# A packed attention followed by a gated feed-forward on one core: the first batch's steps in another order, 99 copies and splits on other engines, and the first softmax's sums in two-column operations

## The chip, the cores and the metric

The kernel runs as one launch on one core of a Trainium2 chip. The core has five engines that matter here: TensorE (PE in the rows, with its weight loads as PEld), VectorE (DVE), ScalarE (ACT), GpSimd (POOL), and SyncE (SP), which issues the DMAs. Each engine works through its own list of instructions in order and waits for the others by semaphores. The metric is the device time of an execution in microseconds; lower is better. The kernel before takes 666.89 us, the median of three runs (666.89 to 667.42).

## The reference

All arrays are float32: 8 batches, 8 heads, 576 positions, 64 channels per head, 32 packed positions, 2048 hidden features.

```python
scale = 1.0 / np.sqrt(q.shape[-1])
def sm_attn(qq, kk, vv):
    s = scale * np.matmul(qq, kk.transpose(0, 1, 3, 2))
    s = s - np.max(s, axis=-1, keepdims=True)
    a = np.exp(s)
    a = a / (np.sum(a, axis=-1, keepdims=True) + 1e-09)
    return np.matmul(a, vv)
p_packed = sm_attn(p, k, v)
out = sm_attn(q, p_packed, p_packed)          # 8 x 8 x 576 x 64
x = out.transpose(0, 2, 1, 3).reshape(8 * 576, 512)
h = x @ w_in                                  # 512 -> 2048
g = h * (1.0 / (1.0 + np.exp(-1.702 * h)))
return g @ w_out                              # 2048 -> 512
```

## The kernel before, in words

**Precision.** The large products need more than one pass of the fast format. An operand is split into an upper half (a copy rounded to fp32r) and a lower half (the difference), and each product is made of three matmuls: upper by upper, upper by lower, lower by upper. The steps whose names end in `_upper` and `_lower` make these halves: an upper half is a copy by `move` (L178 on ScalarE, L180 on the other engines), a lower half is a subtraction (L300 for w_out, L612 for M, L699 for A, L763 and L869 for the hidden features).

**The work of one batch.** `scores1` multiplies p by k (L376), a softmax over the keys follows, its result is turned (for batch 0 by TensorE, L472 and L484, for later batches by VectorE and through a scratch array `aside` in DRAM, `turn1_out` L501 and `turn1_in` L512), and `pack` multiplies it by v (L525; for batch 0 `pack_first`, L545). `scores2_mm` multiplies q by the packed result (L631); its softmax over the 32 packed positions is done on turned blocks (`scores2_turn` L639, `max2` L656, `sub2` L662, `exp2` L666, `sum2` L670 to L672, `norm2` L676, `turn2` L679) and its weights, split, are A (`a_upper`, `a_lower`; for the first part of batch 0 by TensorE and the copies `a_lower_mm`, L692 and L693). `m_chunk` (L597) multiplies the packed result by a chunk of w_in and gives M; `h_mm` (batch 0) and `hp_mm` (later) multiply M by A (L713) and give the hidden features. The gate is `h_tanh` and `h_gate` (L729, L706) for the first four feature blocks and `h_gelu` (L736) or `hp_gelu` (L829) from then on; `out_mm` (L768, batch 0) and `plain` and `product` (L895, later) multiply by w_out into the four accumulators acc.

**The first batch also decodes the weights.** They arrive as 64-bit integers of which the kernel loads the upper words (`load_w`, L266, on SP's queue); `begin_w` (ScalarE, L274) and `join_w` (VectorE, L287) put a float32 together. w_in takes 16 such blocks (numbers 0 to 3, 8 to 11, 16 to 19, 24 to 27), w_out 16 (the others); the first four blocks are loaded in halves. A block's place is loaded again with a later block once it is joined, so `load_w` waits for `join_w`.

**Banks.** PSUM has eight banks: four accumulators acc0 to acc3, h4 and h5 for `h_mm` in turn, and b6 and b7 for the rest. An `h_mm` into a bank waits until the gate of the `h_mm` before it has read that bank.

**What sets the order.** Nothing is scheduled: one tuple named `order` lists 3649 steps in program order, and each step emits its instructions on the engine that it names, or on its default. An engine's list is this tuple restricted to it. Every engine runs ahead of the others as far as its waits allow. The steps `warm` are matmuls of the identity into an unused bank; they keep TensorE at work while nothing else is ready.

**The first softmax.** It takes its maximum over the first 256 keys first, exponentiates these with that maximum (`exp1_first`), corrects by a factor exp(first maximum minus final maximum) (`factor_first`, L431), and `sum1` joins the two partial sums for each of the two head sets eo = 0 and 1:

```python
sm, rs = sm1(eo), rs1(eo)
if b == 0:
    nc.vector.scalar_tensor_tensor(
        sm[:, 0:1], sm[:, 0:1], ff(eo)[:, 0:1], sm[:, 1:2], op0=ALU.mult, op1=ALU.add
    )
nc.vector.tensor_scalar(rs, sm[:, 0:1], 1e-9, 2.0, op0=ALU.add, op1=ALU.mult)
nc.vector.reciprocal(rs, rs)
if b == 0:
    nc.vector.tensor_scalar(ff(eo)[:, 1:2], ff(eo)[:, 0:1], rs, None, op0=ALU.mult)
```

Of the kernel before, what the change touches and what calls it, by code (L numbers as in the profile page):

```python
# [24 lines left out]
def kernel(  # L25
# [527 lines left out]
    def pack_first_half(eo):  # L553
        t = st["bank", "Pf", 0]
        nc.scalar.activation(
            pf[:, eo, :], t[:, eo * D : (eo + 1) * D], AF.Copy, scale=ff(eo)[:, 1:2]
        )
# [393 lines left out]
    def keep_over(n, i, k, engine=nc.sync):  # L951
# [13 lines left out]
        (factor_first, 0), (turn1_first_copy, 0, dve), (factor_first, 1), (exp1_first, 1, 1),  # L965
        (load_w, 2, 1), (sum1, 0, 1), (turn1_first, 1, 7), (load_w, 3, 1), (sum1, 0, 0),
        (turn1_last_mm, 0, 6), (load_w, 4), (turn1_first_copy, 1), (pack_first, 0),
        (turn1_last_copy, 0), (pack_first, 1), (pack_first_half, 0), (pack_first_half, 1),
        (pack_first, 2), (load, 'k', 1, 0), (pack_first_end, 0), (pack_turn_mm, 0, 7),
        (warm, 6, 2, 5), (pack_turn_copy, 0, act), (begin_w, 0, 0), (load_w, 1, 1),  # L970
        (scores2_mm, 0, 0, (6, 7)), (join_w, 0, 0), (warm, 4, 2, 4), (begin_w, 2, 0),
        (load_w, 0, 1), (scores2_turn, 0, 0, 0), (scores2_mm, 0, 1, (2, 3)),
        (scores2_turn, 0, 0, 1), (begin_w, 1, 0), (load, 'k', 1, 1), (max2, 0, 0, 0),
        (warm, 5, 2, 5), (max2, 0, 0, 1), (warm, 8, 3, 4), (load_w, 7), (scores2_turn, 0, 1, 0),
        (sub2, 0, 0, 1, pool), (scores2_turn, 0, 1, 1), (warm, 0, 3, 5), (load_w, 5),
        (sub2, 0, 0, 0, pool), (max2, 0, 1), (load_w, 9), (warm, 2, 3, 4), (exp2, 0, 0, 0),
        (begin_w, 3, 0), (join_w, 2, 0), (exp2, 0, 0, 1), (join_w, 1, 0), (begin_w, 3, 1),
        (sum2, 0, 0, 0), (load_w, 6), (join_w, 3, 0), (norm2, 0, 0, 0, pool),
        (m_chunk, 0, 0, (0, 1), 0), (sum2, 0, 0, 1), (load_w, 8), (m_upper, 0, 0, 1, 0, act),
        (m_upper, 0, 0, 0, 0, act), (sub2, 0, 1, None, pool), (turn2, 0, 0, 0), (load_w, 11),  # L980
        (m_lower, 0, 0, 1, 0), (a_upper, 0, 0, 0, act), (load_w, 10), (a_lower_mm, 0, 0, 0, 6),
        (norm2, 0, 0, 1, dve), (exp2, 0, 1), (join_w, 3, 1), (scores1, 1, 0, (5, 4)),
        (turn2, 0, 0, 1), (begin_w, 4), (sum2, 0, 1), (load_w, 16), (a_upper, 0, 0, 1, act),
        (a_lower_copy, 0, 0, 0), (a_lower_mm, 0, 0, 1, 7), (scores1_copy, 1, 0, 1, act),
        (join_w, 4), (norm2, 0, 1, None, pool), (m_lower, 0, 0, 0, 0), (upper_w, 4, act),
# [1019 lines left out]
```

## Time and profile before

| what | value |
|---|---|
| median of the three runs | 666.89 us |
| the profiled execution's own time | 665.34 us |
| its span (first to last instruction) | 663.6 us |
| TensorE busy, matmul | 653.4 us (98%) |
| VectorE busy | 497.0 us (75%) |
| ScalarE busy | 375.9 us (57%) |
| GpSimd busy | 240.3 us (36%) |
| granted TensorE clock | 1.0 of full speed in every slice |

A busy share on TensorE includes matmuls whose ends are modelled, so a row that is busy throughout may still hold short waits; a wait of a few tenths of a microsecond shows as a note in brackets behind a row, or as a group of matmuls that takes longer than another group of the same count. The first 25 us hold the loads, the first softmax and the first decoding of weights; from then on the rows of TensorE follow each other.

### The profile page before, as it was taken

How to read it: one execution, taken by the hardware profiler on the slowest of the kernel's cores; microseconds unless marked ns; L12 is line 12 of the kernel's file. 1: busy time of each engine (PE TensorE's matmuls, PEld its weight loads, DVE VectorE, ACT ScalarE, POOL GpSimd, SP SyncE). 2: the span in 40 equal slices, each digit the busy share in tenths (PEclk: the TensorE clock that was granted, in tenths of full speed). 3: DMA queues.
4: the chain of work that ended last, by engine and by line, in shares of the span. 5: the costliest groups of instructions: out<-in, count | busy, mean ns of one | idle time of the engine just before them, and what ended most of it. 6: DMA issues, size and time to landing. Idle time of an engine off the chain costs nothing.

```text
span 663.6 us, 15877 instructions
## 1 busy us (share of the span) xinstructions
PE 653.4 (98%) x6136; PEld 594.1 (90%) x6136; DVE 497.0 (75%) x1078; ACT 375.9 (57%) x735; POOL 240.3 (36%) x319
## 2 busy tenths in 40 slices
PE   8999999999999999999999999999999999999997
PEld 6578777899899988999899998899989998899997
DVE  4988786999996577657887658785788558964685
ACT  4886786557884357725646535663657536523430
POOL 2540441154253335342413143462244434444431
PEclk9999999999999999999999999999999999999999
DMA  8998654625553354625632536363545454210231
GB/s 335 417 385 265 220 195 130 177 76 195 174 154 90 112 198 178 156 48 174 245 122 83 141 112 207 112 186 77 177 143 159 100 164 146 79 39 13 82 117 34
DMA packets 94252, 103.14 MB, mean 155 GB/s; under 512 B 69152, under 2 KB 74208, under 8 KB 89568
## 3 DMA queue, kind: packets, MB, share of 16 engines
q1 hardware_dynamic: 94016, 101.86, 49.0%
q8 instruction: 48, 0.79, 0.5%
q14 instruction: 28, 0.23, 0.1%
q10 hardware_dynamic: 160, 0.26, 0.1%
HBM read 80.14 MB, written 21.95 MB: 154 GB/s over the span
## 4 chain that ended last, share of the span: by engine, by line
PE 89%; DVE 1%; ACT 1%; issue 1%; DVEq 0%; ACTq 0%
PE acc L895 47%; PE hh L713 27%; PE acc L768 5%; PE b L597 4%; PE h L713 2%; PE b L525 1%; PE hh L631 1%; PE hh L376 1%; ACT L187 0%; ACT at_float L829 0%; DVE at_float L925 0%; DVE at_float L938 0%; PE b L376 0%; ACT L666 0%; PE h L631 0%
## 5 line engine op out<-in xcount | busy, mean ns | idle before, releaser
L895 PE MATMUL acc<-at_float32r 128*128 128x256 f32 (+1 forms) x2652 | 353.8, 284 | 0.1
L895 PEld LDWEIGHTS acc<-at_float32r 128*128 128x128 f32 x2652 | 331.9, 189 | 22.1 <-issue 14.2
L713 PE MATMUL hh<-at_float32r 128*128 128x288 f32 x1344 | 206.8, 296 | 0.2
L713 PEld LDWEIGHTS hh<-at_float32r 128*128 128x128 f32 x1344 | 185.5, 188 | 3.8 <-issue 0.9
L178 ACT CAST at_float32r<-at_float 128x512 fp32r<-128x512 f32 (+5 forms) x211 | 117.3, 572 | 75.4 <-PE acc L895 48.6
L869 DVE TENSOR_TENSOR at_float32r<-at_float,at_float32r 128x512 fp32r<-128x512 f32 (+3 forms) x186 | 121.4, 663 | 35.5 <-ACT at_float32r L178 31.4
L829 ACT ACTIVATE at_float<-hh 128x576 f32<-128x576 f32 x112 | 73.0, 651 | 131.8 <-PE hh L713 83.7
L869 POOL TENSOR_TENSOR at_float32r<-at_float,at_float32r 128x416 fp32r<-128x416 f32 (+1 forms) x66 | 80.3, 1219 | 103.9 <-ACT at_float32r L178 58.5
L180 DVE CAST at_float32r<-at_float 128x416 fp32r<-128x416 f32 (+5 forms) x125 | 53.1, 430 | 36.8 <-PE acc L895 28.9
L854 POOL TENSOR_TENSOR at_float<-at_float 128x256 f32<-128x256 f32 x49 | 38.0, 778 | 61.5 <-ACT at_float L829 29.6
L854 DVE TENSOR_TENSOR at_float<-at_float 128x256 f32<-128x256 f32 x75 | 35.9, 479 | 25.5 <-ACT at_float L829 19.5
L768 PE MATMUL acc<-at_float32r 128*128 128x512 f32 x192 | 50.7, 397 | 0.1
L858 POOL TENSOR_TENSOR at_float<-at_float 128x128 f32<-128x128 f32 x46 | 24.5, 534 | 61.0 <-DVE at_float L854 45.2
L862 POOL TENSOR_TENSOR at_float<-at_float 128x128 f32<-128x128 f32 x53 | 31.8, 602 | 39.1 <-DVE at_float L858 32.6
L612 DVE TENSOR_TENSOR at_float32r<-b,at_float32r 128x512 fp32r<-128x512 f32 (+1 forms) x64 | 41.7, 669 | 2.1 <-ACT at_float32r L178 2.0
L768 PEld LDWEIGHTS acc<-at_float32r 128*128 128x128 f32 x192 | 34.0, 188 | 9.9 <-issue 2.1
L187 ACT ACT_TABLE_LOAD x33 | 42.3, 1283 | 0.6
L178 ACT CAST at_float32r<-b 128x512 fp32r<-128x512 f32 (+1 forms) x51 | 28.4, 578 | 17.2 <-PE b L597 16.6
L597 PE MATMUL b<-at_float,at_float 64*32 64x512 f32 (+1 forms) x512 | 34.1, 586 | 0.0
L713 PEld LDWEIGHTS h<-at_float32r 128*128 128x128 f32 x192 | 27.8, 188 | 6.5 <-ACT at_float L736 0.9
L858 DVE TENSOR_TENSOR at_float<-at_float 128x128 f32<-128x128 f32 x78 | 23.8, 307 | 11.9 <-POOL at_float L854 11.2
L713 PE MATMUL h<-at_float32r 128*128 128x256 f32 (+1 forms) x192 | 30.7, 300 | 1.1 <-ACT at_float L736 0.4
(128 smaller groups left out, 570.3 us busy)
## 6 DMA issues: line engine op xcount, KB each, us to landing
at_float<-w_kept SPq DMA_DIRECT2D x24, 1024.0 KB, 5.3
at_float<-v SPq DMA_DIRECT2D x8, 1024.0 KB, 5.8
o<-at_float SPq DMA_DIRECT2D x32, 256.0 KB, 2.5
at_float<-w_out SPq DMA_DIRECT2D x16, 511.8 KB, 6.3
at_float<-q SPq DMA_DIRECT2D x14, 576.0 KB, 4.8
at_float<-w_in SPq DMA_DIRECT2D x12, 511.8 KB, 9.0
at_float<-k_last SPq DMA_DIRECT2D x8, 640.0 KB, 6.1
at_float<-pk SPq DMA_DIRECT2D x8, 576.0 KB, 6.1
```

The lines of the kernel that those rows point to most:

```text
L178: nc.scalar.copy(dst, src)
L180: engine.tensor_copy(dst, src)
L187: nc.scalar.activation(small("table", 1), ident[:, :1], func)
L597: nc.tensor.matmul(banks[eo][32 * j : 32 * j + 32, columns(part)], pt(b)[rows(eo), j, :], w[rows(eo), j, columns(part)], start=True, stop= ...
L612: nc.vector.tensor_tensor(lo, t[:, at], hi.bitcast(F32), op=ALU.subtract)
L713: nc.tensor.matmul(t[:, : halves(b)[half]], m_part(fc, eo, mp)[:, fo : fo + P], a_part(b, half, ap, eo), start=(n == 0), stop=(n == len(te ...
L768: nc.tensor.matmul(acc[i], g0(f, gp)[:, i * P : (i + 1) * P], wo(f, wp), start=(start and n == 0), stop=(stop and n == 2),)
L829: nc.scalar.activation(g, h, AF.Gelu_apprx_sigmoid, scale=2.0)
L854: engine.tensor_tensor(dst, src, by, op=ALU.subtract)
L858: engine.tensor_tensor(g_raw(n, p, 6), g_raw(n, p, 5), g_raw(n, p, 1), op=ALU.add)
L869: engine.tensor_tensor(lo, src, g_range(n, p, 0, which)[0].bitcast(F32), op=ALU.subtract)
L895: nc.tensor.matmul(acc[i][:, at : at + m], lhs, rhs, start=(start and k == 0), stop=(stop and k == len(pairs) - 1),)
```

## The change

Three things change. The sums of the first softmax are laid side by side, so that both head sets are treated by one instruction of two columns: five operations (`sums_first`) stand where eight stood, and the factors (`factor_first`) follow the last exponential instead of standing ahead of it.

```diff
+    def sums_first():
+        sm, rs, f = small("sm1", 4), small("rs1", 2), small("ff", 4)
+        nc.vector.tensor_tensor(sm[:, 0:2], sm[:, 0:2], f[:, 0:2], op=ALU.mult)
+        nc.vector.tensor_tensor(sm[:, 0:2], sm[:, 0:2], sm[:, 2:4], op=ALU.add)
+        nc.vector.tensor_scalar(rs, sm[:, 0:2], 1e-9, 2.0, op0=ALU.add, op1=ALU.mult)
+        nc.vector.reciprocal(rs, rs)
+        nc.vector.tensor_tensor(f[:, 2:4], f[:, 0:2], rs, op=ALU.mult)
...
-        (factor_first, 0), (turn1_first_copy, 0, dve), (factor_first, 1), (exp1_first, 1, 1),
-        (load_w, 2, 1), (sum1, 0, 1), (turn1_first, 1, 7), (load_w, 3, 1), (sum1, 0, 0),
...
+        (exp1_first, 1, 1), (turn1_first_copy, 0, dve), (factor_first, 0), (factor_first, 1),
+        (load_w, 2, 1), (turn1_first, 1, 7), (load_w, 3, 1), (sums_first,), (turn1_last_mm, 0, 6),
```

The first 700 steps of `order`, the first batch and the beginning of the next round, stand in another order; the 2948 steps behind them are the same, on the same engines. Among the loads, the second half of w_in's block 0 goes ahead of the keys of batch 1, the blocks 27, 25 and 24 move, and the second batch's values and queries are loaded later than before. TensorE's list has the same 1257 steps, and the last 1086 of them stand as before.

Copies, splits and a few other steps of that first part, 106 in all, move to another engine: 33 from VectorE to GpSimd, 24 from VectorE to ScalarE, 22 from ScalarE to VectorE, 14 from ScalarE to GpSimd, 13 from GpSimd to one of the two. GpSimd gets 22 rounding copies (CAST) to fp32r, which it had none of. ScalarE's list has two table loads fewer.

VectorE, 16 to 20 us into the program: at_float_116, 118 and 135 are raw blocks 2, 1 and 3 of w_in, `sum2` is the three instructions from L670 (L676 after), `turn2` L679 (L685 after), and the results go to at_float_244 (240 after). Before:

```order
L287 SCALAR_TENSOR_TENSOR at_float_244<-at_float_116,at_float_83 128x256
L287 SCALAR_TENSOR_TENSOR at_float_244<-at_float_118,at_float_83 128x256
L670 TENSOR_REDUCE at_float_89<-at_float_250 128x8
L671 TENSOR_SCALAR at_float_89<-at_float_89 128x8
L672 RECIPROCAL at_float_89<-at_float_89 128x8
L287 SCALAR_TENSOR_TENSOR at_float_244<-at_float_135,at_float_83 128x256
L670 TENSOR_REDUCE at_float_89<-at_float_250 128x8
```

and in the changed kernel, behind `join_w` of block 2 and the first `sum2`:

```order
L662 TENSOR_REDUCE at_float_89<-at_float_260 128x20
L287 SCALAR_TENSOR_TENSOR at_float_240<-at_float_135,at_float_83 128x256
L685 STREAM_TRANSPOSE at_float_295<-at_float_252 128x256
L676 TENSOR_REDUCE at_float_89<-at_float_252 128x8
L677 TENSOR_SCALAR at_float_89<-at_float_89 128x8
L678 RECIPROCAL at_float_89<-at_float_89 128x8
L287 SCALAR_TENSOR_TENSOR at_float_240<-at_float_118,at_float_83 128x256
```

The join of block 1 has moved from ahead of the first `sum2` to behind the second one and `turn2`; the join of block 3 is now ahead of it.

TensorE, about 41 to 46 us: h_72 and h_73 are the banks h4 and h5, acc_63 to acc_66 the accumulators acc0 to acc3. The first row of either list is feature block 6, the 128x320 row the second half of block 4, the next h_72 row its first half, the last row block 5. Before:

```order
L713 MATMUL h_72<-at_float32r 128x256 x6
L768 MATMUL acc_65<-at_float32r 128x512 x3
L713 MATMUL h_73<-at_float32r 128x320 x6
L768 MATMUL acc_66<-at_float32r 128x512 x3
L768 MATMUL acc_65<-at_float32r 128x512 x3
L713 MATMUL h_72<-at_float32r 128x256 x6
L713 MATMUL h_73<-at_float32r 128x256 x6
```

and in the changed kernel:

```order
L719 MATMUL h_72<-at_float32r 128x256 x6
L719 MATMUL h_73<-at_float32r 128x320 x6
L774 MATMUL acc_63<-at_float32r 128x512 x3
L719 MATMUL h_72<-at_float32r 128x256 x6
L774 MATMUL acc_66<-at_float32r 128x512 x3
L719 MATMUL h_73<-at_float32r 128x256 x6
```

Between two uses of bank h4 there are now one `h_mm` and one `out_mm`, where one `h_mm` and three `out_mm` stood.

ScalarE, the same stretch: L448 (L451) is the exponential of batch 1, L729 (L735) `h_tanh`, L274 `begin_w`, L736 (L742) `h_gelu` with its table load; at_float_325 (396) is the place of block 14 of the weights. Before:

```order
L448 ACTIVATE at_float_133,at_float_89<-at_float_133,at_float_89 128x576
L729 ACTIVATE at_float_352<-h_73 128x256
L274 CAST at_float_83<-at_float_325 128x512
L178 CAST at_float32r<-at_float_352 128x256
L736 ACT_TABLE_LOAD
L736 ACTIVATE at_float_352<-h_72 128x256
L736 ACTIVATE at_float_352<-h_73 128x320
```

and in the changed kernel:

```order
L735 ACTIVATE at_float_333<-h_73 128x256
L451 ACTIVATE at_float_133,at_float_89<-at_float_133,at_float_89 128x576
L742 ACT_TABLE_LOAD
L742 ACTIVATE at_float_333<-h_72 128x256
L274 CAST at_float_83<-at_float_396 128x512
L742 ACTIVATE at_float_333<-h_73 128x320
```

`begin_w` of block 14 has moved from ahead of the table load to behind the first `h_gelu`.

## Rows read from the trace of the kernel before

**Rows 1.** The page, busy time of each engine, share and instructions.

```profile
PE 653.4 (98%) x6136; PEld 594.1 (90%) x6136; DVE 497.0 (75%) x1078; ACT 375.9 (57%) x735; POOL 240.3 (36%) x319
```

**Rows 2.** Busy us by engine in a stretch: length, PE, PEld, DVE, ACT, POOL.

```profile
20.00:30.00 10.00, 9.25 (x84) 5.78 (x84) 9.57 (x24) 8.14 (x20) 4.93 (x5) 1.00 1.02 417
```

**Rows 3.** Timeline of PE, first 25 us: start, length, instruction, idle before it.

```profile
18.44 0.62 PE L597 MATMUL acc<-at_float,at_float 64*32 64x256 f32 x4 [0.42 <-DVE at_float L287]
19.52 0.70 PE L692 MATMUL b<-at_float,at_float 128*128 128x256 f32 x2 [0.46 <-DVE at_float L679]
...
22.41 0.39 PE L713 MATMUL h<-at_float32r 128*128 128x256 f32 x1 [0.16 <-ACT at_float L178]
23.21 1.64 PE L713 MATMUL h<-at_float32r 128*128 128x256 f32 x11 [0.42 <-DVE at_float32r L612]
```

**Rows 4.** Timeline of PE, 38 to 52 us.

```profile
38.79 2.23 PE L768 MATMUL acc<-at_float32r 128*128 128x512 f32 x9
...
45.13 1.69 PE L713 MATMUL h<-at_float32r 128*128 128x256 f32 x12 [0.44 <-ACT at_float L736]
46.65 0.86 PE L768 MATMUL acc<-at_float32r 128*128 128x512 f32 x3
47.35 0.87 PE L713 MATMUL h<-at_float32r 128*128 128x256 f32 x6
48.06 2.59 PE L768 MATMUL acc<-at_float32r 128*128 128x512 f32 x9
```

**Rows 5.** Timeline of ACT, 38 to 52 us.

```profile
42.34 0.79 ACT L274 CAST at_float<-at_float 128x512 f16<-128x512 bf16 x1 [1.44 <-DMA at_float<-w_out]
...
43.40 1.28 ACT L736 ACT_TABLE_LOAD   x1
```

**Rows 6.** Timeline of DVE, first 30 us.

```profile
9.48 0.22 DVE L453 SCALAR_TENSOR_TENSOR at_float<-at_float 128x1 f32<-128x1 f32 x1 [0.38 <-ACT at_float L440]
...
10.88 0.21 DVE L459 TENSOR_SCALAR at_float<-at_float 128x1 f32<-128x1 f32 x1
...
13.18 0.43 DVE L287 SCALAR_TENSOR_TENSOR at_float<-at_float,at_float 128x256 uint32<-128x256 uint32 x1 [1.16 <-ACT at_float L274]
...
18.30 0.41 DVE L670 TENSOR_REDUCE at_float<-at_float 128x8 f32<-128x256 f32 x1
...
19.51 0.42 DVE L612 TENSOR_TENSOR at_float32r<-acc,at_float32r 128x256 fp32r<-128x256 f32 x1
...
22.75 0.41 DVE L612 TENSOR_TENSOR at_float32r<-acc,at_float32r 128x256 fp32r<-128x256 f32 x1
```

**Rows 7.** Timeline of DVE, 47 to 51 us.

```profile
48.49 0.68 DVE L300 TENSOR_TENSOR at_float32r<-at_float,at_float32r 128x512 fp32r<-128x512 f32 x1
```

**Rows 8.** Timeline of ACT, first 30 us.

```profile
8.47 0.47 ACT L431 ACTIVATE at_float<-at_float 128x1 f32<-128x1 f32 x2
...
14.08 0.49 ACT L274 CAST at_float<-at_float 128x256 f16<-128x256 bf16 x1 [0.99 <-DMA at_float<-w_in]
```

**Rows 9.** Groups of POOL by form: count, busy us, mean ns, idle before.

```profile
L180 POOL COPY at_float<-at_float 128x64 f32<-128x64 f32 x44 | 14.3, 325 | 37.0 <-ACT at_float L829 30.4 <-issue 6.4
L763 POOL TENSOR_TENSOR at_float32r<-at_float,at_float32r 128x256 fp32r<-128x256 f32 x16 | 13.7, 859 | 22.6 <-DVE at_float32r L180 15.7 <-DVE at_float L456 3.2 <-ACT at_float32r L178 2.6
...
L662 POOL TENSOR_TENSOR at_float<-at_float,at_float 128x256 f32<-128x256 f32 x2 | 1.2, 616 | 11.7 <-DVE at_float L656 11.7
```

**Rows 10.** Groups of DVE by form, 4 to 165 us.

```profile
L763 DVE TENSOR_TENSOR at_float32r<-at_float,at_float32r 128x256 fp32r<-128x256 f32 x16 | 6.9, 442 | 0.0
```

**Rows 11.** Timeline of SP, 43 to 72 us.

```profile
59.28 0.91 SPq L501 DMA_DIRECT2D aside<-at_float  x1
...
66.07 2.97 SPq L512 DMA_DIRECT2D at_float<-aside  x6
```

**Rows 12.** DMA issues, 65 to 69 us: count, KB each, median us to landing.

```profile
at_float<-aside SPq DMA_DIRECT2D x2, 32.0 KB, 2.8
```

**Rows 13.** Timeline of PE, 66 to 78 us.

```profile
72.17 1.32 PE L525 MATMUL b<-at_float,at_float 128*32 128x64 f32 x80
```

More of the change, by code (lines that the diff above doesn't have):

```diff
@@ L976 @@
[L976 to L985, printed above, removed]
-        (a_lower_copy, 0, 0, 1, dve), (begin_w, 1, 1), (scores1_copy, 1, 0, 0, dve),
-        (begin_w, 0, 1), (h_mm, 0, 0, 0, 4), (lower_w, 4, pool), (turn2, 0, 1), (h_mm, 0, 1, 0, 5),
@@ new lines @@
+        (h_tanh, 0, 2, 0), (lower_w, 5, pool), (h_over, 0, 1, pool), (join_w, 9), (join_w, 6),
+        (begin_w, 8), (h_over, 0, 0, act), (h_gate, 0, 2, 0), (bias1, 1, 1), (out_mm, 0, 1, 0),
+        (begin_w, 10), (upper_w, 6, act), (out_mm, 0, 1, 1), (join_w, 11),
+        (h_lower, 0, 1, 1, pool), (h_mm, 0, 2, 1, 5), (h_tanh, 0, 2, 1), (join_w, 8),
+        (h_mm, 0, 3, 1, 4), (exp1, 1, 1), (join_w, 10), (out_mm, 0, 1, 2),
+        (m_chunk, 0, 1, (6, 7), None), (h_tanh, 0, 3, 1), (h_upper, 0, 2, 0, act),
@@ new lines @@
+        (h_upper, 0, 8, 1, act), (turn1_in, 1, 0), (load, 'q', 1, 0), (h_lower, 0, 8, 1, dve),
+        (over_out, 2), (out_mm, 0, 6, 2), (h_mm, 0, 9, 1, 5), (lower_w, 21, dve),
+        (h_over, 0, 8, pool), (h_gelu, 0, 10, 0), (join_w, 25), (out_mm, 0, 8, 2), (load_w, 29),
+        (h_mm, 0, 11, 0, 4), (h_gelu, 0, 9, 1), (h_over, 0, 9, dve), (lower_w, 22, dve),
+        (h_upper, 0, 9, 1, pool), (h_upper, 0, 9, 0, pool), (load, 'q', 1, 1),
+        (h_lower, 0, 9, 0, dve), (pack, 1, (6, 7)), (begin_w, 28), (join_w, 27), (pack_end, 1),
@@ new lines @@
+        (m_chunk, 1, 1, (6, 7), None), (out_mm, 0, 12, 1), (join_w, 31), (h_mm, 0, 13, 0, 5),
+        (norm2, 1, 0, None, pool), (out_mm, 0, 12, 3), (sum2, 1, 1), (out_mm, 0, 11, 3),
+        (h_gelu, 0, 14, 1), (m_upper, 1, 1, 1, None, act), (m_upper, 1, 1, 0, None, dve),
+        (h_upper, 0, 14, 0, act), (over_out, 4), (turn2, 1, 0), (h_upper, 0, 14, 1, pool),
+        (a_upper, 1, 0, None, act), (upper_w, 31, pool), (h_lower, 0, 14, 1, pool), (win_out, 0),
+        (h_gelu, 0, 13, 0), (m_lower, 1, 1, 1), (h_upper, 0, 13, 0, act), (m_lower, 1, 1, 0),
@@ L1277 @@
+        (keep, 4, 0), (sums_2, 5, 1, dve), (take_5, 4), (sums_3, 5, 1, pool), (pack, 3, (6, 7)),
+        (rest, 5, 2, pool), (g_upper, 5, 1, 1, act), (hp_over, 5, 2), (g_lower, 5, 1, 1, pool),
+        (pack_end, 3), (load, 'q', 3, 0), (product, 5, 0, 2), (product, 5, 0, 4), (keep, 4, 1),
         (pack_turn_mm, 3, 6), (product, 5, 1, 1), (g_upper, 5, 2, 0, dve),
@@ L1319 @@
[L1319 to L1323 removed]
+        (both, (scores2_mm, 3, 0, (4, 5)), (m_chunk, 3, 0, (6, 7), None)),
@@ new lines @@
+        (both, (scores2_mm, 3, 1, (4, 5)), (m_chunk, 3, 1, (6, 7), None)),
+        (g_lower, 5, 4, 1, dve), (table_for, AF.Exp, 9), (exp2, 3, 0), (sums_3, 5, 5, dve),
+        (g_upper, 5, 5, 0, dve), (rest, 5, 6, act), (sum2, 3, 0), (hp_over, 5, 6),
+        (product, 5, 3, 7), (win_in, 3, 2), (product, 5, 4, 7), (load, 'k', 4, 0),
+        (scores2_turn, 3, 1, 1), (product, 5, 4, 1), (norm2, 3, 0, None, pool),
+        (table_for, AF.Gelu_apprx_sigmoid, 10), (m_upper, 3, 1, 1, None, act), (product, 5, 4, 3),
```

1122 lines of the change are left out of this document (559 added, 563 removed).

## The prediction

> **What bounds the kernel.** I read the page first: TensorE's matmuls cover 98% of the span and its weight loads 90% [rows 1]. So time can only come from places where TensorE waits or does stopgap work. Next the timeline of TensorE: the reader is to see where a bracket stands behind a row, and where a group of matmuls takes longer than another of the same count. In the first 24 us the brackets are many; the last ones name VectorE (a join of w_in, then M's lower half) and ScalarE (the copy that frees bank h4) [rows 3]. VectorE is busy 9.57 of the 10 us from 20 to 30, TensorE 9.25 [rows 2]. After that only two losses are left in the first batch. At 45.13 `h_mm` of block 4 waits 0.44 for the gate of block 6 [rows 4]; rows that follow without a wait overlap by 0.16 (46.65 + 0.86 against 47.35), so the wait costs 0.44 + 0.16 = 0.60. At 48.06 nine `out_mm` matmuls take 2.59 where nine others take 2.23 [rows 4]: 0.36 lost. The rest of the 663.6 us is one row behind the other. The most that a reordering can win behind 24 us is therefore 0.60 + 0.36 = 0.96 us, and I look at the start by itself.
>
> **The change, part by part.**
>
> *The same work on TensorE.* Its list holds the same matmuls in both kernels, the same 13 groups of small packed matmuls among them, and its last 1086 steps stand as they did. What it does costs the same; only waits can differ, and what it is ahead or behind at the end of the first 700 steps, it keeps to the end.
>
> *First softmax.* Before, eight operations on one column run from 9.48 to 10.88 + 0.21 = 11.09 [rows 6], 1.61 us or 0.20 each. Five of them are 1.01. The two factors (0.47 together [rows 8]) now stand behind the last exponential instead of ahead of it: that one starts some 0.25 earlier (half of the 0.47; it is then held by its own bias), and the sums start later, about when they did. They end some 0.5 earlier. They were not alone on the path, since `pack_first` and the copies ahead of it are still to come, so I take the 0.25 of the exponential as the lead at 13 us: the block of idle time of 1.16 before the join at 13.18 [rows 6] shrinks, and that join now fits into it.
>
> *What the lead is worth.* Nothing at once: `begin_w` of block 2 waits for its DMA at 14.08 and ends at 14.57 [rows 8]; the transfers ahead of it are the same in both kernels. Its join now stands right behind the first maximum, about 0.3 before VectorE would otherwise have got there, and VectorE waits about as long as it led. From there to 22.75, M's last lower halves, it has the same operations to do.
>
> *The join of block 1.* This is the step with a price. `m_chunk` needs the joins of blocks 0 to 3 and TensorE waits for the last of them until 18.44 [rows 3]. In the new order the last one stands behind a `sum2` and a `turn2` which before came right after it: from 18.30 to 19.51 [rows 6], 1.21 us. So the join ends near 19.6 instead of 18.4 and `m_chunk`, with twelve matmuls left instead of four, near 20.5 instead of 18.44 + 0.62 = 19.06. From there to the first `h_mm` TensorE needed 22.41 - 19.06 = 3.35, of which 0.46 and 0.16 were waits [rows 3]: 2.73 of work. 20.5 + 2.73 = 23.23. Before, the first `h_mm` issued one matmul at 22.41 and the other five from 23.21, held by M's lower half (22.75 + 0.41 = 23.16 [rows 6]). So the waits of before cover most of the delay, and about 0.25 is left: the second matmul at some 23.45 against 23.21. Bounds: if the softmax's lead survives and the DMA does not hold VectorE, 0.3 is won; if nothing covers the 1.21, and ScalarE's queue (now with both of M's upper halves behind two copies) adds nothing, 1.0 is lost. I take +0.25, between the ends, because it follows the rows.
>
> *The waits at 45 and 48 us.* The first has a clear cause: ScalarE idles 1.44 until 42.34 for the DMA of block 14 of the weights, `begin_w` of it being ahead of the table load at 43.40, and the gate comes behind the load [rows 5]. In the new order the table load and the gate come first and `begin_w` behind them. TensorE now asks for bank h4 sooner, one `h_mm` and one `out_mm` after block 6 (some 1.6 us by the rows of 0.87 and 0.86 [rows 4]) instead of after four steps, but the gate needs only that its matmuls are done. The 0.60 goes. The second wait is for the lower half of block 12 of the weights on VectorE (48.49 + 0.68 = 49.17 [rows 7]); it now stands before the joins of 16 and 13, and the `out_mm` that needs it comes at the same point: the 0.36 goes. Together -0.96.
>
> *Moved copies.* They are worth nothing as long as TensorE does not wait for the engine they leave, which it does not between 24 and 44 us. What they cost depends on GpSimd, where 22 rounding copies are new. The trace has none: below them stands a copy of 64 columns, 325 ns; above, a subtraction of 256 columns with two inputs, 859; the nearest is the plain subtraction of 256, 616 [rows 9]. I take 0.6 us for 256 columns, 1.2 for 512. Counted over the steps that stand beside TensorE's work from 31 to 39 us, these durations make some 6.7 us of GpSimd's work in 8. On the longest chain (a copy, three lower halves, and one of w_out at 512 columns: 0.6 + 3 x 0.86 + 1.3 = 4.5) it is never idle. The `out_mm` that reads them come some 1.7 us later than they are ready, which hides them; at the upper end the chain grows by 0.3 and is still hidden. I allow 0.25 for new waits of this kind anywhere in 700 steps, an estimate from the size of the two that are there now.
>
> A remark on moving work that way: the Trainium skill (Perfetto Trace Analysis, Optimizing Scalar/DVE Operations) warns that GpSimd and VectorE share a port into SBUF, so that shifting operations between those two might not help. The trace has the same subtraction at 859 on GpSimd and 442 on VectorE [rows 9, 10], and does not show by itself how much of it is sharing. By the rule the moved copies would come nearer to 0.86 each and the sum would be the same, since the 1.7 us still cover them.
>
> **Sum.** +0.25 - 0.96 + 0.25 = -0.46 us, on the profiled execution 665.34 to 664.9; the median of the runs lies 1.55 above that execution, so 666.89 becomes 666.4. A measurement here can tell about 0.2%, 1.3 us, from no change; so this is no change.
>
> **The rivals.**
>
> *The start gains as well (faster).* If block 1's join is not late, and the 0.25 to 0.5 of the softmax is carried through, and no new wait comes: -0.5 - 0.96 = -1.5, 665.4; a little more if the last waits around 25 us go too. For it: VectorE is the bound there and has lost two copies from 23 us on. Against: the DMA at 14.08 and the order of the joins. Chance 0.17.
>
> *Pack comes too early for its transfers (slower).* The second batch's `pack` starts at 72.17 [rows 13]; its operands come back from DRAM by six transfers issued from 66.07 to 69.04, which land 2.8 us after their issue, the last near 71.4 [rows 11, 12]. That is 0.7 of slack. In the new order four `out_mm` of 0.69 that stood before `pack` stand behind it, so TensorE asks 2.8 us sooner, near 69.4 less what the waits of before give back, 68.5. Against that the turned blocks go out earlier in SP's list, before two loads of q and one of weights that stood ahead of them; the last went out at 59.28 [rows 11], and I expect it some 4 us sooner. But SP works in order, and in its new list these stores stand behind loads of blocks 20 to 23, which wait for joins on VectorE. It decides whether the last transfer is issued before 65.7. If it is at 68.6 as before, TensorE waits 71.4 - 68.5 = 2.9: -0.46 + 2.9 = +2.4, 669.3. Chance 0.13.
>
> *GpSimd is late (slower or none).* If the copies take 0.95 and the lower halves lengthen to 1.1, the chain of 4.5 becomes about 5.5, still inside its 1.7 of cover; waits begin only when it starts 0.7 late as well, and each wait then is some tenths. Three or four of them cost 1.5: 667.9. Chance 0.10, half of it beyond the bound.
>
> **Chances and range.** The forecast, 666.4 with its own range of 665.7 to 667.6: 0.60. Faster by over 0.2% is the first rival's greater part and a tail: 0.15. Slower: the pack, half of GpSimd's case, and a tail of orders whose waits I have not found: 0.19. Within: 0.66. The range that leaves out two in ten: 665.0 to 669.0.
>
> **What would show it.** Right: the row of the first eleven `h_mm` matmuls near 23.4; no bracket and no long group at 44 to 49 us; the table load ahead of `begin_w` of block 14; `pack` without a bracket near 69; rounding copies of 0.5 to 0.9 on GpSimd. Wrong: brackets on `m_chunk` beyond 20 us that push the first `h_mm` past 24, a bracket of microseconds on `pack` with a DMA as its cause, or GpSimd named behind `out_mm`.

## The result, and the profile after

The changed kernel takes 671.46 us (median of six runs, 669.86 to 673.02) where the kernel before, beside it, takes 666.89. The two medians make 1.0069; the ratio given with the runs, which is used below, is 1.0075, 95% interval [1.0065, 1.0085]. So the change makes the kernel slower by some 0.7%. The profiled execution took 671.26 (span 669.5), 5.92 more than that of before.

Busy times hardly differ from [rows 1], except that GpSimd has 21 us more. The page after:

```profile
PE 655.3 (98%) x6136; PEld 596.0 (89%) x6136; DVE 494.1 (74%) x1052; ACT 371.1 (55%) x722; POOL 261.2 (39%) x353
```

So I read stretches. Busy us by engine (length, PE, PEld, DVE, ACT, POOL, then the granted clock of TensorE, 1.00 being 2.4 GHz, and the DMA share), first by tens, then by twos:

```profile
20.00:30.00 10.00, 9.30 (x74) 5.57 (x75) 7.96 (x20) 7.68 (x19) 5.59 (x6) 0.83 1.03 417
40.00:50.00 10.00, 10.00 (x60) 8.91 (x59) 8.19 (x19) 7.84 (x16) 5.29 (x8) 1.00 0.93 318
70.00:80.00 10.00, 6.51 (x123) 4.44 (x122) 2.48 (x7) 2.89 (x7) 1.31 (x3) 0.83 0.86 292
...
18.00:20.00 2.00, 0.00 (x0) 0.00 (x0) 1.93 (x7) 1.38 (x4) 1.65 (x2) 1.00 1.04 420
20.00:22.00 2.00, 1.73 (x15) 0.83 (x15) 1.97 (x6) 1.69 (x3) 0.40 (x1) 0.53 1.04 426
22.00:24.00 2.00, 2.00 (x22) 0.78 (x20) 0.98 (x3) 0.53 (x2) 1.39 (x1) 0.62 1.03 420
24.00:26.00 2.00, 1.79 (x9) 1.05 (x7) 1.48 (x3) 2.00 (x7) 0.50 (x2) 1.00 1.00 401
...
76.00:78.00 2.00, 2.00 (x6) 1.51 (x6) 0.41 (x2) 1.29 (x3) 0.00 (x0) 0.50 1.01 405
```

The first row answers to [rows 2]: VectorE is no longer the engine that is full. In two stretches TensorE works at 1.2 GHz, each right behind a stretch in which it did nothing. Against that, 40 to 50 us is full: TensorE's two losses there are gone. The timeline of TensorE says the same in brackets (start, length, instruction, idle before it; line numbers are 6 higher than before):

```profile
17.29 0.62 PE L603 MATMUL acc<-at_float,at_float 64*32 64x256 f32 x4
20.27 1.09 PE L603 MATMUL acc<-at_float,at_float 64*32 64x256 f32 x12 [2.36 <-DVE at_float L287]
21.30 1.22 PE L698 MATMUL b<-at_float,at_float 128*128 128x256 f32 x2
...
24.54 1.41 PE L719 MATMUL h<-at_float32r 128*128 128x256 f32 x6
...
46.88 2.23 PE L774 MATMUL acc<-at_float32r 128*128 128x512 f32 x9
...
73.51 1.32 PE L531 MATMUL b<-at_float,at_float 128*32 128x64 f32 x80 [3.48 <-DMA at_float<-q]
74.77 1.65 PE L774 MATMUL acc<-at_float32r 128*128 128x512 f32 x3
...
79.21 1.06 PE L603 MATMUL b<-at_float,at_float 64*32 64x512 f32 x16
```

`m_chunk` waits 2.36 for a join instead of 0.42 [rows 3], and at half clock the two matmuls at 21.30 take 1.22 instead of 0.70. The nine `out_mm` at 46.88 take 2.23, where those of [rows 4] took 2.59, and no `h_mm` has a bracket there. `pack`, which stood at 72.17 without a wait [rows 13], waits 3.48, and the three `out_mm` behind it take 1.65 (0.96 at full clock, see below). The transfer named behind `pack` is not the cause: it landed after 73.51. The profile's list of waits has the weight load of the same line, which names turn1_in:

```profile
PEld b L531 <- DMA at_float<-aside: 3.7, 1, 3.7
```

SP's queue and its transfers (timeline: issue and length; then KB each and median us to landing; then SP's waits from 60 to 70 us):

```profile
60.40 0.60 SPq L507 DMA_DIRECT2D aside<-at_float  x1
61.04 0.62 SPq L222 DMA_DIRECT2D at_float<-v  x1
64.28 1.99 SPq L518 DMA_DIRECT2D at_float<-aside  x4
66.38 0.36 SPq L266 DMA_DIRECT2D at_float<-w_out  x1
66.79 0.89 SPq L518 DMA_DIRECT2D at_float<-aside  x2
...
at_float<-v SPq DMA_DIRECT2D x1, 1024.0 KB, 8.9
at_float<-aside SPq DMA_DIRECT2D x4, 128.0 KB, 6.3
...
at_float<-aside SPq DMA_DIRECT2D x2, 32.0 KB, 5.9
...
SPq L518 <- DMA aside<-at_float: 2.5, 1, 2.5
```

The last turned block went out at 60.40, behind it 1 MB of `v`, and behind that the six transfers that `pack` needs. These took 5.7 to 6.7 us to land; before, the two small ones took 2.8 [rows 12] and the four large ones 3.1. So what was late is not the turned block. It went out later than before but landed sooner (64.27 against 65.98), and the last transfer back for `pack` went out at 67.26 instead of 68.61; behind `v`, though, it landed at 73.47 instead of 71.43. Ahead of the turned block SP itself waited 1.4 for a lower half on GpSimd and 0.8 for a join.

### The profile page after: what moved, and what is told of

The parts are those of the page before. It is cut to its first block, busy times and chain, and to the rows that moved or that the text cites. A ratio compares the mean times of both kernels' runs of the same rounds, so it can differ in the third digit from the quotient of the medians.

```text
span 669.5 us, 15884 instructions
## 1 busy us (share of the span) xinstructions
PE 655.3 (98%) x6136; PEld 596.0 (89%) x6136; DVE 494.1 (74%) x1052; ACT 371.1 (55%) x722; POOL 261.2 (39%) x353
## 4 chain that ended last, share of the span: by engine, by line
PE 89%; DMA 5%; ACT 2%; DVE 2%; SPq 1%; issue 1%; POOL 0%; DVEq 0%; ACTq 0%; POOLq 0%
PE acc L901 46%; PE hh L719 25%; PE acc L774 6%; PE b L603 4%; PE h L719 3%; DMA at_float<-q 2%; DMA at_float<-w_in 2%; PE b L531 1%; DMA at_float<-v 1%; PE hh L637 1%; PE hh L376 1%; ACT at_float32r L178 0%; ACT L187 0%; DMA at_float<-aside 0%; PE b L376 0%
## 5 line engine op out<-in xcount | busy, mean ns | idle before, releaser
L178 ACT CAST at_float32r<-at_float 128x512 fp32r<-128x512 f32 (+5 forms) x206 | 115.5, 575 | 80.2 <-PE acc L901 52.8
L875 POOL TENSOR_TENSOR at_float32r<-at_float,at_float32r 128x512 fp32r<-128x512 f32 (+3 forms) x67 | 81.7, 1223 | 107.4 <-ACT at_float32r L178 50.9
L180 DVE CAST at_float32r<-at_float 128x512 fp32r<-128x512 f32 (+3 forms) x108 | 47.9, 447 | 40.1 <-PE acc L901 28.7
L603 PE MATMUL b<-at_float,at_float 64*32 64x512 f32 (+1 forms) x512 | 33.9, 586 | 0.0
```

What stands on the lines that cost most here:

```text
L178: nc.scalar.copy(dst, src)
L180: engine.tensor_copy(dst, src)
L603: nc.tensor.matmul(banks[eo][32 * j : 32 * j + 32, columns(part)], pt(b)[rows(eo), j, :], w[rows(eo), j, columns(part)], start=True, stop= ...
L875: engine.tensor_tensor(lo, src, g_range(n, p, 0, which)[0].bitcast(F32), op=ALU.subtract)
```

## The experiments

Every edit is one of steps in the tuple `order`; a diff shows where a step goes, and where it stood if that isn't plain. "Above" means above the kernel before, in us: the ratio less one, times 666. By this the changed kernel is 5.0 above; the expectations say 4.6, from the two medians. The intervals reach 0.6 to 1.4 us to either side; where two overlap, no difference between the runs is shown.

### The joins, v, both, and stopgap matmuls

One repair for each of the two waits, both together, and a kernel that leaves all waits for data in place and fills TensorE's idle time. The edits are on the changed kernel.

```diff
 (join_w, 3, 0),
+(join_w, 1, 0),
 (sub2, 0, 1, None, pool),
...
 (sum2, 0, 0, 1),
-(join_w, 1, 0),
```

> The changed kernel (671.46, 4.6 above the kernel before) with one step moved: the join of weight block 1 stands right behind that of block 3, ahead of the turn and the sums of the second softmax. Theory (the join is what holds m_chunk): TensorE goes on in m_chunk near 18.5 us instead of 20.27, the granted clock of 20 to 30 us is 1.0 instead of 0.83, the first h_mm stands near 22.8 instead of 24.54, and the time falls by about 2 to 669.4. Rival 1 (the front is late because VectorE and ScalarE have other copies and another order as well): the first h_mm stays beyond 24, 671.4. Rival 2 (pack is held by transfers that do not move with TensorE): the front gains 2 and the wait at pack grows from 3.5 to 5.5, 671.4.

Measured: 1.0057 [1.0045, 1.0069], 3.8 above; 1.2 won, not 2. The clock of 20 to 30 us was 1.00, but the join did not come at 18.5: `m_chunk` waited until 19.58. The wait at `pack` did not grow to 5.5, as the second rival had it; it was 2.62, with the half clock behind it. VectorE's and GpSimd's timelines in this kernel, then TensorE's at `pack`:

```profile
17.68 1.84 DVE L287 SCALAR_TENSOR_TENSOR at_float<-at_float,at_float 128x256 uint32<-128x256 uint32 x2
...
17.84 1.40 POOL L668 TENSOR_TENSOR at_float<-at_float,at_float 128x640 f32<-128x640 f32 x1
...
71.95 2.36 PE L531 MATMUL b<-at_float,at_float 128*32 128x64 f32 x80 [2.62 <-DMA at_float<-aside]
```

Two joins of 0.43 take 1.84, and end 0.28 behind GpSimd's subtraction (19.52 against 19.24). The changed kernel has the same at a smaller operation. There the 8-column `TENSOR_SCALAR` of 0.17 takes 0.46, as long as GpSimd's subtraction lasts (18.25 to 19.65), and the join stands behind it:

```profile
18.81 0.37 DVE L676 TENSOR_REDUCE at_float<-at_float 128x8 f32<-128x256 f32 x1
19.22 0.46 DVE L677 TENSOR_SCALAR at_float<-at_float 128x8 f32<-128x8 f32 x1
...
19.83 0.38 DVE L287 SCALAR_TENSOR_TENSOR at_float<-at_float,at_float 128x256 uint32<-128x256 uint32 x1
...
18.25 1.40 POOL L668 TENSOR_TENSOR at_float<-at_float,at_float 128x640 f32<-128x640 f32 x1
```

```diff
 (load_w, 18),
+(load, 'v', 1, 0),
...
 (turn1_out, 1, 0, 2), (join_w, 24),
-(load, 'v', 1, 0),
```

> The changed kernel with one step moved: the load of v for the second batch (1 MB) stands behind the load of weight block 18 on SP's queue, some 30 us earlier, instead of between the last turn1_out and the first turn1_in. Theory (pack waits for v and for what v's packets hold up): turn1_in lands near 70, the wait of 3.5 at pack falls under 0.5, the granted clock of 70 to 80 us is 1.0 instead of 0.83, and 3.5 + 1.4 = 4.9 go: 666.5. Rival (pack comes too early for turn1_in whatever v does): a wait of 1 to 2 stays, 668.5 to 669.

Measured: 1.0018 [1.0002, 1.0033], 1.2 above: 3.8 of the 5.0 won, the largest part of the loss. A wait of 1.77 at `pack` stayed, as the rival had it, now without a lower clock behind it. The last two of its transfers, issued behind block 28 of the weights, took 3.9 and 4.0 us to land, the first four 2.5 to 3.1. At the front, `m_chunk` waited 3.60 in this execution, with the same front as the changed kernel's 2.36, because a block of w_in landed late (15.49 instead of 14.45), and the clock fell behind that wait:

```profile
21.20 0.65 PE L603 MATMUL acc<-at_float,at_float 64*32 64x256 f32 x12 [3.60 <-DVE at_float L287]
...
72.59 1.32 PE L531 MATMUL b<-at_float,at_float 128*32 128x64 f32 x80 [1.77 <-DMA at_float<-aside]
```

```diff
 (join_w, 3, 0),
+(join_w, 1, 0),
...
 (load_w, 18),
+(load, 'v', 1, 0),
```

> The changed kernel with both moves (join of block 1 behind that of block 3; v early). If front and pack are the two costs, and apart from each other: 671.46 - 2.1 - 4.9 = 664.5, which is 2.4 under the kernel before. If the 2 us won ahead of pack make it wait for turn1_in again: a wait of 1 to 2 at pack and 666 to 667.

Measured: 1.0038 [1.0024, 1.0052], 2.5 above, more than either number that I had expected, and not shown to be better or worse than v alone (the intervals overlap). In its profiled execution `m_chunk` waits 2.07 and `pack` 0.97, both at full clock; what keeps the median up, this run does not show.

```diff
+(warm, 9, 10, 4),
 (m_chunk, 0, 0, (0, 1), 0),
...
+(warm, 10, 15, 6),
 (pack, 1, (6, 7)),
```

> The changed kernel with stopgap matmuls of 128 columns into free banks: 10 ahead of m_chunk, where it waits 2.36 us, and 15 ahead of pack, where it waits 3.5. All waits for data stay; only the idle time is filled. If the lower granted clock behind these waits (0.83 of 10 us, twice) costs time by itself: both windows at 1.0, and 0.5 to 1 us at the front and 1.4 behind pack come back, 669.1 to 669.6. If the slower matmuls only stand where TensorE would wait anyway: 671.5.

Measured: 1.0033 [1.002, 1.0046], 2.2 above: 2.8 won by stopgap work that computes nothing. Timeline and windows:

```profile
19.49 1.41 PE L603 MATMUL acc<-at_float,at_float 64*32 64x256 f32 x16
...
23.04 1.41 PE L719 MATMUL h<-at_float32r 128*128 128x256 f32 x6
...
20.00:22.00 2.00, 1.87 (x33) 0.84 (x31) 1.97 (x6) 1.77 (x4) 0.40 (x1) 1.00 1.02 410
```

The last twelve matmuls of `m_chunk` start at 20.24, as in the changed kernel (20.27), but the first `h_mm` starts at 23.04 instead of 24.54. So 1.5 of the front's delay is the half clock, and not the wait, by one execution of each.

### GpSimd's subtraction, three repairs, pack alone, sums alone

The first two are edits on the changed kernel, the other two on the kernel before (whose line numbers the row of the third has).

```diff
 (join_w, 3, 0),
+(join_w, 1, 0),
-(sub2, 0, 1, None, pool),
+(sub2, 0, 1, None, dve),
```

> The changed kernel with the join of block 1 behind that of block 3, as in the run before (there 3.7 above the kernel before), and one engine more: the subtraction sub2(0, 1) of 640 columns goes from GpSimd to VectorE, behind the join. In the run before, the join of block 1 took 1.48 instead of 0.42, from 18.05 to 19.52, and ended 0.28 after GpSimd's subtraction (17.84 to 19.25). Theory (VectorE's operation with two inputs in SBUF stands still while GpSimd's runs): the join takes 0.42, m_chunk goes on near 18.5 instead of 19.57, its wait falls from 1.43 to 0.4, and VectorE gets about 0.95 of work in place of the 1.06 that it lost; the time falls by about 1, to 2.7 above the kernel before. Rival (the join waits for its own data): it takes 1.4 or starts later, and nothing changes, 3.7 above.

Measured: the mechanism as expected, the time not: 1.0074 [1.0056, 1.0093], 4.9 above. VectorE, then TensorE:

```profile
17.82 0.78 DVE L287 SCALAR_TENSOR_TENSOR at_float<-at_float,at_float 128x256 uint32<-128x256 uint32 x2
...
18.65 0.65 PE L603 MATMUL acc<-at_float,at_float 64*32 64x256 f32 x12 [1.00 <-DVE at_float L287]
19.75 0.70 PE L698 MATMUL b<-at_float,at_float 128*128 128x256 f32 x2 [0.44 <-DVE at_float L685]
...
22.86 0.39 PE L719 MATMUL h<-at_float32r 128*128 128x256 f32 x1 [0.38 <-ACT at_float32r L178]
...
71.12 2.15 PE L531 MATMUL b<-at_float,at_float 128*32 128x64 f32 x72 [2.49 <-DMA at_float<-aside]
```

Both joins take 0.78 in place of 1.84, and `m_chunk` goes on 0.93 sooner. But new brackets follow (the turned softmax, ScalarE's copies), and the first `h_mm` comes only 0.2 sooner than with GpSimd's subtraction (22.86 against 23.05). What TensorE led, it lost at `pack`, at half clock: 80 small matmuls of 1.32 take over 2. By their intervals this run and the one with GpSimd's subtraction (3.8 above) are not apart.

```diff
 (join_w, 3, 0),
+(join_w, 1, 0),
-(sub2, 0, 1, None, pool),
+(sub2, 0, 1, None, dve),
...
 (load_w, 18),
+(load, 'v', 1, 0),
...
+(turn1_in, 1, 5), (turn1_in, 1, 0),
 (load_w, 28),
```

> The changed kernel with three edits: join of block 1 early and sub2(0, 1) on VectorE, v for the second batch early, and the last two turn1_in ahead of the load of weight block 28 on SP's queue. If the join behind GpSimd's subtraction, v, and that load are what made the change slower: m_chunk's wait near 0.4, pack's under 0.3, the granted clock 1.0 in every 10 us, and what is left of the change is its gain at 45 and 48 us: 1 us under the kernel before, 0.9985 of it. If something else in the new order costs: above the kernel before by over 1 us, with waits at other places than these two.

Measured: 1.0011 [1.0001, 1.0021], 0.7 above, not 1 under. No wait at the first `pack`, clock 1.00 throughout, but one place that I had not listed, the next batch's `pack`:

```profile
147.55 1.32 PE L531 MATMUL b<-at_float,at_float 128*32 128x64 f32 x80 [0.58 <-DMA at_float<-aside]
```

```diff
 (h_mm, 0, 11, 0, 4),
+(pack, 1, (6, 7)),
...
 (out_mm, 0, 10, 1),
-(pack, 1, (6, 7)),
```

> The kernel before with one step moved: pack stands ahead of the four out_mm of 0.69 that stood before it, where the changed kernel has it; v is early, as it was. Its last turn1_in lands at 71.43, and pack would start at 72.17 - 2.76 = 69.41. Theory (pack waits for turn1_in, whatever v does): a wait of 2.0 at pack, and 2.0 to 3.4 above the kernel before (the larger where the granted clock falls behind the wait). Rival (only v's late load makes pack wait): no wait, 0.

Measured: 1.0029 [1.0019, 1.0039], 1.9 above. In the old order of SP's queue `pack` is too early even with `v` where it was:

```profile
71.32 1.49 PE L525 MATMUL b<-at_float,at_float 128*32 128x64 f32 x80 [1.36 <-DMA at_float<-aside]
```

```diff
-(sum1, 0, 1),
...
-(sum1, 0, 0),
+(sums_first,),
```

> The kernel before with the two-column sums alone, in the place of the second of the two one-column sums: five operations instead of eight, and in no other place. The prediction took the lead for lost at the next transfers: 0 against the kernel before, within 0.3. If the softmax is on the path of the front: 0.5 under it. If one operation for both halves waits for the later half, and this holds pack_first: up to 0.5 above.

Measured: 1.0004 [0.9996, 1.0013]: nothing, as forecast.

### The priced gain alone, v late alone, the engines back

The first three are edits on the kernel before, the second on top of the first; the last is one on the kernel with three repairs.

```diff
-(begin_w, 14),
...
 (h_gelu, 0, 6, 0),
+(begin_w, 14), (join_w, 14),
...
 (upper_w, 12, dve),
+(lower_w, 12, dve),
```

> The kernel before with only the two edits that the prediction priced at 0.96: the high halves and the join of weight block 14 stand behind the table load and the gate of block 6, and the lower half of block 12 of the weights stands ahead of the joins of 16 and 13. The rows say: no wait at 45.13 and no long out_mm at 48.06, pack some 0.9 sooner, at 71.3. If the 0.96 lasts to the end: 0.9 under the kernel before. If what is ahead waits for transfers at pack (its last operand landed at 71.43) or later: 0 to 0.4 under it.

Measured: 1.0014 [1.0005, 1.0023], 0.9 above, not 0.9 under. The wait at 45 us is gone, and two of the same size stand right behind it:

```profile
49.27 0.96 PE L768 MATMUL acc<-at_float32r 128*128 128x512 f32 x3 [0.43 <-DVE at_float32r L763]
50.66 0.50 PE L768 MATMUL acc<-at_float32r 128*128 128x512 f32 x1 [0.43 <-POOL at_float32r L763]
```

What was a wait for the gate became one for the lower halves that follow the gate. The two edits that I priced do not give the 0.96; the changed kernel has it through its whole order.

```diff
-(load_w, 28),
...
 (turn1_in, 1, 4),
+(load_w, 28),
```

> The same two edits, and the load of weight block 28 (512 KB) behind the first four turn1_in on SP's queue instead of ahead of them, so that pack's operands do not follow it: turn1_in lands near 70 instead of 71.4, pack waits for nothing. If the gain of the two edits was lost at pack: 0.9 to 1.0 under the kernel before, the fastest of all here. If it is lost later: as the run before.

Measured: 1.0065 [1.005, 1.0079], 4.3 above: block 28 was due itself. ScalarE waited 3.16 for it, until 74.84; behind `pack`, TensorE waits 2.29 for a lower half that comes after it on ScalarE's list, at 78.20, and goes on at half clock. The run says nothing on the question it was made for.

```diff
-(load, 'v', 1, 0),
...
 (turn1_out, 1, 0, 1),
+(load, 'v', 1, 0),
```

> The kernel before with one step moved: the load of v for the second batch stands behind the last turn1_out, where the changed kernel has it; pack stays behind its four out_mm. v would be issued near 60 instead of 40.9 and land near 68; turn1_in is issued from 66.07 as before, and has v's last packets and one block of w_out ahead of it. If v's late load costs by itself: turn1_in lands at 72.5 to 73.5, a wait of 0.4 to 1.3 at pack, 0.5 to 2 above the kernel before. If it costs only together with an early pack: no wait, 0.

Measured: 1.0036 [1.0024, 1.0048], 2.4 above; v's late load costs by itself, the wait just beyond the 1.3, and the time beyond the 2, that I expected (the bracket names block 28, which landed at 71.79, sooner than the last turn1_in at 73.67):

```profile
73.73 0.48 PE L525 MATMUL b<-at_float,at_float 128*32 128x64 f32 x19 [1.37 <-DMA at_float<-w_out]
```

```diff
-(a_upper, 0, 0, 1, pool),
+(a_upper, 0, 0, 1, act),
...
-(rest, 2, 6, pool),
+(rest, 2, 6, act),
```

> The kernel with three edits (join of block 1 early with sub2(0, 1) on VectorE, v early, two turn1_in ahead of block 28), which was 0.7 above the kernel before, and on top every other copy and split of the changed kernel back on the engine that it had before; the order of the steps stays as changed. If the moved copies cost and win nothing, as the prediction has it: the same time within 0.7. If GpSimd's share (its busy time of 30 to 40 us went from 5.2 to 7.5) holds VectorE up: 1 or more under the run with three edits. If the new order needs the new engines: waits between 24 and 66 us and some microseconds more.

Measured: 1.0149 [1.0136, 1.0162], 9.9 above, 9.2 more than the same order with the new engines. VectorE is full in 30 to 40 and 50 to 60 us (9.97 of 10), and TensorE waits for its lower halves and for ScalarE's copies:

```profile
93.44 1.42 PE L774 MATMUL acc<-at_float32r 128*128 128x512 f32 x5 [0.88 <-DVE at_float32r L300]
...
102.16 1.09 PE L603 MATMUL b<-at_float,at_float 64*32 64x512 f32 x16 [0.84 <-DVE at_float32r L618]
```

### What the front still costs, and where the gain goes

The first stands on the kernel with three repairs, the second on top of it; then the two edits on SP's queue alone, in the changed kernel, and stopgap matmuls on top of those.

```diff
+(begin_w, 1, 0),
 (begin_w, 3, 0),
...
+(join_w, 1, 0),
 (join_w, 3, 0),
```

> The kernel with three edits (0.7 above the kernel before), and the join of weight block 1 now ahead of that of block 3, with its copy on ScalarE, as in the kernel before: m_chunk takes the blocks in the order 0 to 3, so that four matmuls are left behind the last join instead of twelve. Theory (this is what the front still costs, once GpSimd's subtraction is out of the joins' way): the wait in m_chunk falls from 1.0 to 0.5 or less, the first h_mm stand near 22.4 and 23.2 instead of 22.86 and 23.74, 0.5 is won: 0.2 above the kernel before. Rival (something else at the front costs): 22.8 and 23.7, 0.7 above.

Measured: 1.0001 [0.9992, 1.0009]: no difference from the kernel before, nearer to the theory in time, but not by its path: the wait in `m_chunk` fell to 0.67, and the first `h_mm` came at 22.77, as the rival had it, again behind new brackets.

```diff
+(load, 'v', 2, 0), (load, 'v', 2, 1),
 (hp_mm, 2, 1, 1),
```

> As the run before, and v for the third batch loaded some 30 us earlier on SP's queue, where the kernel before has it. In the kernel with three edits the second pack waits 0.58 at 147.6 for turn1_in, whose last issue follows a turn1_out that landed only behind v (138.1 and 140.6). Theory (the 1 us won at 45 and 48 us is given back there): no wait at 147.6, 0.4 to 0.6 under the run before, and 0.2 to 0.4 under the kernel before. Rival (v fills nothing but waits anyway further on): no difference to the run before.

Measured: 1.0068 [1.0047, 1.0088], 4.5 above: a miss. At its new place v held up the stores behind it. The first of them took 5.91 to land (2.4 in the run before), VectorE waited 4.35 for it, until 113.55, and TensorE got the wait below behind ScalarE's exponentials. That the gain is lost at the second `pack` is therefore not shown by repairing it, only by rows (below):

```profile
119.01 1.85 PE L719 MATMUL hh<-at_float32r 128*128 128x288 f32 x12 [2.77 <-ACT at_float L835]
```

```diff
 (load_w, 18),
+(load, 'v', 1, 0),
...
+(turn1_in, 1, 5), (turn1_in, 1, 0),
 (load_w, 28),
```

> The changed kernel with only the two edits on SP's queue (v for the second batch early, two turn1_in ahead of block 28); the front stays as changed. This leaves the front's cost alone: no wait at pack, the wait of 2.4 in m_chunk with the lower clock behind it. By the theory of two separate costs: the changed kernel less 4.9, which is 0 to 1.5 above the kernel before, since 2.1 of the front stand against the 1.1 won at 45 and 48 us and 0.5 given back later. If the front's delay is made up before pack: at or under the kernel with three edits (0.7 above).

Measured: 1.0017 [1.0006, 1.0027], 1.1 above, as two separate costs would have it, though the interval holds the 0.7 of the other expectation too. Its profiled execution was the fastest of its twelve, 665.45, at full clock:

```profile
19.72 0.65 PE L603 MATMUL acc<-at_float,at_float 64*32 64x256 f32 x12 [1.68 <-DVE at_float L287]
...
22.52 1.42 PE L719 MATMUL h<-at_float32r 128*128 128x256 f32 x6
...
67.94 1.32 PE L531 MATMUL b<-at_float,at_float 128*32 128x64 f32 x80
69.19 0.96 PE L774 MATMUL acc<-at_float32r 128*128 128x512 f32 x3
...
72.30 1.06 PE L603 MATMUL b<-at_float,at_float 64*32 64x512 f32 x16
```

Here `m_chunk` is 1.3 later than before, and still the first `h_mm` is through no later than before: all six from 22.52 to 23.94, where [rows 3] had one at 22.41 and the next from 23.21. Its twelve executions take 665.45 to 668.90; the five with a mean clock of 0.998 or more are on average 1.5 faster than the others (666.48 against 667.95). `pack` starts at 67.94 without a wait, 4.2 sooner than before.

```diff
+(warm, 9, 9, 4),
 (m_chunk, 0, 0, (0, 1), 0),
```

> The kernel with only the two repairs on SP's queue (in its profiled execution the wait in m_chunk was 1.68, the clock stayed at 1.0 and the first full h_mm stood at 22.86; its times scatter from 665.5 to 668.9), and 9 stopgap matmuls of 128 columns (0.21 each, 1.9 together) ahead of m_chunk, to fill that wait. Theory (the front's cost is above all the half clock, in those executions whose wait is long): the times draw together near the lowest, 665.5 to 666.5, at or up to 0.5 under the kernel before. Rival (the scatter and the cost come from when data arrives): the same scatter and the same median, 0.9 above.

Measured: 1.0015 [1.0006, 1.0024]: the scatter falls (665.61 to 667.83, clocks 0.998 to 1.000), the median does not; the filling seems to cost what it saves. In its profiled execution the wait behind the nine is another 1.6, since a block of w_in came late.

```diff
+(warm, 9, 12, 4),
 (m_chunk, 0, 0, (0, 1), 0),
```

> As the run before with 12 stopgap matmuls (2.6 us), which reaches over the longest wait seen at full arrival (2.36) but delays m_chunk by some 0.6 where the wait is 1.7. Theory: scatter as small, median 0 to 0.6 above the run with 9. If 9 are too few for the long waits: this one is faster than the run with 9.

Measured: 1.0005 [0.9995, 1.0015], no difference from the kernel before, and the lowest single time of all (664.77), but no version here is shown to beat it. Nor is it shown to be faster than the one with 9: the intervals overlap.

## Why the prediction was wrong

The forecast was no change, 666.4, with a range of 665.0 to 669.0; the change took 671.46. By the profiled executions: the front +1.9 (its first six `h_mm` end at 25.95; before at 24.06, with the fifth of the eleven that [rows 3] has from 23.21), the waits at 45 and 48 us -0.96, `pack` +3.48, and the half clock behind it +1.34 (`pack` to the next L603 takes 5.70; in the kernel with SP's queue repaired, 4.36). That is 5.8. The traces agree at points where both kernels have done the same matmuls: the changed one is 1.9 behind after the first six `h_mm`, 0.6 at 54 us (1.3 won, 0.96 of it these two waits), 5.6 at 79 us and 5.8 at 148; it ends 5.9 behind. Two waits later (0.18 and 0.50, at 171.8 and 236.6) are made up again within 20 us.

**The decisive step: the rival with pack.** In the sum `pack` stood at nothing; it cost 3.48 and the half clock 1.34. What I gave 0.13 is what happened. Its own test held: the last two turn1_in went out from 66.79 on, not before 65.7. Three things in it were wrong. I expected the turned blocks some 4 us sooner; the last went out at 60.40, behind 59.28 [rows 11], though it landed 1.7 sooner. I did not count v among the steps that SP's list moves, though its load went from ahead of the turned blocks to behind them: it costs 1.37 by itself, as `pack`'s earlier place costs 1.36 by itself, and both together 3.48. And I priced a wait by its length alone, which left out the half clock. The early place as such is not the cost: with `v` early and all six transfers ahead of block 28, `pack` starts at 67.94 and waits for nothing. What costs is the order on SP's queue.

**The front, +0.25, was mis-sized.** The join ended at 20.21 instead of 19.6, and the twelve matmuls behind it take 0.65 at full clock, not 0.9. VectorE stood still 0.3 for GpSimd, and it had waited 0.5 for block 2 of w_in, which landed at 14.45; in the execution of 665.45 that block landed at 14.02, VectorE did not wait for it, and the same join ended at 19.67, with GpSimd in its way as well. So the 19.6 holds for a block in time, and I had no term for a late one. The three traces with the new front as it is have waits of 1.68, 2.36 and 3.60 in `m_chunk`, with the block at 14.02, 14.45 and 15.49. In the six traces of the old order the block landed between 13.93 and 14.22, and the wait was 0.42 or 0.43. Whether the new order makes the block late now and then, no run here shows. The delay alone would not have cost much: with every wait for data in place and the idle time filled, six `h_mm` end at 24.45, +0.4; in the execution of 665.45 at 23.94, -0.1. The waits of before do cover the delay, as I argued, while the clock stays up. In the changed kernel it fell behind the wait, and that is 1.5 of the 1.9.

**The waits at 45 and 48 us, -0.96, went** in the changed kernel as predicted. But the reason was incomplete: the two edits that I named only shift the wait. And the lead does not last. The kernel with three repairs leads by 0.8 at 54 us and 0.4 at 112, waits 0.58 at the next `pack`, and is 0.25 behind after it. It is not only a lead given back: with the joins in order as well, TensorE is 0.6 behind and waits 0.50 there all the same. `v` for the third batch has slipped like that of the second. Before, it went out at 108.16 and the last turned block landed at 133.14; in the kernel with three repairs, 132.47 and 140.58.

**The moved copies "are worth nothing"**: wrong for this order. Their durations were well bounded (527 ns and 808 ns for 256 and 512 columns, against 0.6 and 1.2 us taken), and TensorE does not wait for GpSimd between 24 and 66 us; but without the move the new order, with three repairs, is 9.2 slower. I had asked what they cost on the new engine, not what the old ones would have had to carry.

**Sharing a port.** The prediction left open how much of GpSimd's long durations is sharing. It shows on the other side: VectorE's join of 0.43 lasted 1.48 beside GpSimd's subtraction, and 0.41 without it. The Trainium skill (SBUF — State Buffer, SBUF: two separate sides) calls the port pair an exclusive lock, held for a whole instruction, against a VectorE operation with two inputs in SBUF or in a two-port mode. The traces agree: the join and the 8-column operation last to the end of GpSimd's (that the latter was in such a mode, no row shows), while transposes and reductions between them run at their usual 0.43 and 0.37. I cited the rule for the copies' durations and did not apply it to the queue whose end I was computing.

**The sums** were worth nothing, as forecast.

## What to carry to other kernels

In a reordering, list each queue's moved transfers too, the large ones first: 1 MB that slips between a store and the load which waits for it cost as much wait here as a step taken too early (1.37 and 1.36). A wait on TensorE has two prices, its length and the clock behind it; where the new order makes one wait of two microseconds out of several of 0.4, count both. A lead that is won ahead of a DRAM round trip is only worth what that round trip has in slack. And where a wait hangs on when a load lands, one trace is not enough: the same front had 1.68, 2.36 and 3.60.

## What was not expected of the hardware

The granted clock fell to 1.2 GHz behind waits of 2.36 and 3.48 us in the changed kernel and came back within some 4 us; in other runs it fell behind 2.29, 2.49, 2.62 and 3.60. It did not fall behind 1.68, 1.77 and 2.07, nor behind the 2.77 at 119 us, so the length of the wait alone does not decide it. In the kernel with SP's queue repaired the mean clock of the twelve executions goes from 0.994 to 1.000. One GpSimd subtraction of 640 columns, 1.40 us long, stretched a VectorE operation of 8 columns from 0.17 to 0.46, and a join by 1.06.
